# A linear-attention and MLP block on one core: tile 4 turned by moves, earlier normalisation of tiles 6 and 7, and other reorderings

## The chip, the core and the metric

The kernel runs on one core of a Trainium2 chip. The metric is the device time of one execution in microseconds. The engines work side by side, each in its own program order, and wait for each other by semaphores: TensorE (PE in the profile; its weight loads are PEld), VectorE (DVE), ScalarE (ACT), GpSimd (POOL) and SyncE (SP), which here issues nearly all transfers.

## What is computed

The input x is 2048 tokens by 512. With xn the layer-normalised x, the output is the sum of three parts:

```python
xn = _layernorm(x, axis=-1)
return x + _A_ref(xn, A_wqkv, A_wo) + _B_ref(xn, B_w1, B_b1, B_w2, B_b2)
```

A is linear attention with 32 heads of 16: q, k, v are xn times a 512 x 1536 matrix; phi(t) is t + 1 for positive t and exp(t) otherwise; for each head kv = phi(k)^T v and z = the sum of phi(k) over all tokens, and each token's output is phi(q) kv / (phi(q) z), times a 512 x 512 matrix. B is an MLP: the square of relu(xn w1 + b1), 1376 wide, times w2, plus b2. All is in float32.

## The kernel before

Tokens are worked in 16 tiles of 128, four tiles to a block. Every matmul of the accurate kind is done in three passes: an operand is split into a high part (rounded by a ScalarE or VectorE copy) and a low part (the difference, a subtraction), and high x high, high x low and low x high are accumulated. So each operand needs a copy on one engine and a subtraction on another before TensorE can use it.

The program order of each engine is the order in which the code issues its operations; there is no scheduler (a manual schedule). Names with numbers below are tiles of memory: xp is the normalised tile, pt its transpose in PSUM, xs0 and xs1 the transposed high and low parts (h and l) of two blocks, pk the projection of k and later its parts, k the value of phi, tok the normalised tile's parts, kx the accumulated product of tok and pk.

**First stage, the start (lines 516 to 655).** The first four tiles of x and the k weights are loaded. For each tile VectorE takes mean and variance (`measure`, lines 230 to 235), the root of the variance is made by an addition and a power (`roots`, lines 242 to 246: the addition on VectorE for tiles 0 and 1, else on GpSimd, the power on GpSimd), and `normalise` (248 to 273) writes xp: on VectorE for tiles under NPE = 8, later on ScalarE. A tile is turned in one of two ways:

- for tiles under NDVE = 5, by TensorE (`turned_pe`, line 303): four transposes with the identity into a PSUM bank pt, from which `high` (ScalarE, line 324), `low` (VectorE, line 327) and `keep_t` (a ScalarE copy, stored to DRAM as xTd for later) take their parts;
- for tiles from NDVE on, by moves: `regroup` (line 277) stores the normalised tile to DRAM (via), `move` (line 286) loads it back in four pieces in another order (xg), and `turn` (line 291) has VectorE transpose it within 32 x 32 blocks.

Before the token loop, tiles 0 to 3 are normalised; the loads of tiles 8 to 15 are issued together on SyncE; tiles 4 and 5 are measured as one group (`soon = group(4, 5)`), whose root is taken after the parts of tiles 0 and 1.

**The token loop (line 794 on), i from 2 to 15.** Each iteration issues the moves that are pending (`move()`, line 799), the projection of tile i (12 matmuls, line 369), phi of it (`phi_k`: two ScalarE passes, with the turned tile's `high` between them, then `low` and a VectorE pass), normalises the next group, splits k (`parts`, lines 372 to 377: a ScalarE copy and a VectorE difference) and the next tile's tokens (`tokens`: a ScalarE copy and a GpSimd subtraction), turns tile i + 2 by moves, measures later tiles, and ends with kx(i - 1): 12 matmuls (line 389) in three groups of four, ordered by which parts they need. At i = 5, four small loads of b1 are issued on SyncE (lines 796 to 798), ahead of the moves.

**Between token loop and main stage (lines 867 to 930).** Sums and differences of token blocks and of weight chunks are prepared for a product scheme in which TensorE needs fewer products than blocks: T[1] to T[4] are the token differences, S and aop the weight chunks' sums and parts. The heads' values and the matrix m are made from kx.

**Main stage (line 932 on).** For each half n (two blocks of four tiles) and each step p (a pair of 128-wide units of q or of the MLP, loop in line 1056) the code issues products into PSUM banks A, B and C, with ScalarE copies of A and C (c, t), the last sums' parts of T[3] and T[4] (`last_sums`, from line 1119), the weights' parts, and the second MLP product into acc. In step (0, 0) the parts of T[3] are made after the copy t of bank C.

Of the kernel before, what the change touches and what calls it, by code (L numbers as in the profile page):

```python
# [7 lines left out]
F32 = mybir.dt.float32  # L8
# [5 lines left out]
P = 128  # L14
# [4 lines left out]
def kernel(  # L19
# [39 lines left out]
    BT = TB * P  # L59
    NF = -(-F // P)  # L60
    NPE = 2 * TB
    NDVE = NPE - 3
    WARM = 11
    NP = NF // 2
    FP = NF * P
# [176 lines left out]
    def roots(tiles, st, mv, y):  # L242

        n = len(tiles)
        (nc.vector if tiles[0] < 2 else nc.gpsimd).tensor_scalar(y[:, 1, :n], mv[:, :n, 1], 1e-5, None, op0=OP.add)
        nc.gpsimd.tensor_tensor(out=y[:, 0, :n], in0=y[:, 1, :n], in1=power[:, :n], op=OP.pow)

    def normalise(tiles, st, mv, y):
# [96 lines left out]

        nc.gpsimd.memset(xp[i][:, D - 1:] if i < NDVE else xp[i][:, NJ - 1, P - 1:], 1.0)

    def tokens(i):
        tok[i] = pair(f"tok{i}")
        h, l = tok[i][:, 0], tok[i][:, 1]  # L350
        src = xp[i]
        if i >= NDVE:
            h, l, src = gjc(h), gjc(l), src.rearrange("p g (j c) -> p g j c", j=NJ)
        split(h, l, src, "act", "pool")
        if NDVE <= i + 1 < NT:
            ones(i + 1)

# [23 lines left out]
        phi(ps, kp[i], mid, late)  # L381

    def kx(i):
        second, third = ((1, 0), (0, 1)) if i < 2 else ((0, 1), (1, 0))
        order = (((1, 0),), ((0, 0), (0, 1))) if i >= NPE else (((0, 0),), (second,), (third,))
        todo = [(c, u, v) for group in order for c in range(NJ) for u, v in group]
        first, last = order[0][0], order[-1][-1]
        for c, u, v in todo:
            nc.tensor.matmul(kxp[c], lhsT=tok[i][:, u, c * P:(c + 1) * P], rhs=pk[i][:, v],  # L389
                             start=i == 0 and (u, v) == first, stop=i == NT - 1 and (u, v) == last)  # L390
# [155 lines left out]
    for i0 in range(0, NT, TB):  # L546
        a = first_xp[i0]
        for k in range(TB):
            xp[i0 + k] = a[:, k]
        if i0 + TB <= NDVE:  # L550
            continue
        n = TB if i0 >= NPE else TB // 2
        if i0 < NPE:
            i = i0 + TB - n - 1
            one = work.tile([P, 512], F32, name=f"xg{i}", tag="r0")
            xp[i], xg[i] = (t.rearrange("p (g n) -> p g n", g=NJ) for t in (xp[i], one))
            groups[i] = [xp[i], xg[i]]
# [27 lines left out]
    for t in two_tiles:  # L585
        measure(t)
        roots(*t)
    normalise(*two_tiles[0])
    high, low, keep0 = transposed(0, 2)
    high()  # L590
    heads_k(0, eng="dve")
# [47 lines left out]
    load_x(8, x8[:, :2])  # L639
    load_x(10, x8[:, 2:])  # L640
    load_x(12, two("x12"))
    load_x(14, two("x14"))
    project(2, pks[2], wk, HL)
    soon = group(4, 5)
    normalise(*fourth)
    phi_k(0, pks[0])
    measure(soon, 0)
    tokens(0)
    parts(0)
    phi_k(1, pks[1])  # L650
    tokens(1)
    measure(soon, 1)
    parts(1)
    roots(*soon)
    keep2()

# [135 lines left out]
    kxp = [bank(f"kx{c}", "acc") for c in range(NJ)]  # L792
    kx(0)
    for i in range(2, NT):
        if i == 5:
            nc.sync.dma_start(b1s[:, :NF - 1], b1[:(NF - 1) * P].rearrange("(f p) -> p f", p=P))
            for a, o, n in units(NF - 1):
                nc.sync.dma_start(b1s[a:a + n, NF - 1:], b1[o:o + n, None])
        move()
        if i in (4, 7):  # L800

            b = i // 7
            for u in range(2):
                nc.sync.dma_start(xsd[b][u], f32(cols(b * TB)[u]))
        if i == 9:
            load_o()
        if i > 10:
            fetch()
        ps = pks[i] if i < 3 else bank(f"pk{i}")
        if i > 2:  # L810
            project(i, ps, wk, HL)
        high = low = keep_t = lambda: None
        if i < NDVE:
            high, low, keep_t = transposed(i + 1)

        soon_turned = transposed(i + 2) if 11 <= i and i + 2 < NT else ()

        def mid():
            high()
            more(i)  # L820

        def late():
            low()
            more(i)

        if i == 12:
            rawz = raw_1(NF - 1)
            T.update({n: tokens_sum(n, f"B{n - 1}") for n in (1, 2)})
        if i == 12:
            w = load_1("q", 0)  # L830
        if i == 13:
            todo_1 = operands_first(0, w)
            extra.append(todo_1.pop(1))
        if i == 14:
            z = pair("w1z0")
            extra.append(lambda: split(z[:, 0], z[:, 1], rawz, "act", "dve"))
            o34 = halves(four("Tf", "r0"))
            extra.extend(sums_of(xT[NB - 1], xT[NB - 2], *o34))
            lows = [extra.pop() for k in range(2)]
            extra += [todo_1[0], lows[1], todo_1[1], lows[0], *todo_1[2:]]  # L840
        phi_k(i, ps, mid, late)
        more(i)
        run(*soon_turned)
        later = normalise(*soon) if soon else []
        parts(i)
        keep_t()
        if i == 2:
            tokens(2)
        if i + 1 < NT:
            tokens(i + 1)  # L850
        run(*later)
# [12 lines left out]
        kx(i - 1)  # L864
        more(i)
# [66 lines left out]
    for n in range(2):  # L932
# [118 lines left out]
        def step(k=1):  # L1051

            for _ in range(k):
                do(steps[t1] or steps[t2])

        for p in range(NO + 1):
            at_p = AT[p]
            kind, k = order[p] if p < NO else ("", 0)
# [22 lines left out]
            if kind:  # L1081
# [6 lines left out]
                if kind == "w":  # L1088
                    relu(c11, c11, fa)
                else:  # L1090
                    steps[t1] += steps_of(t1, fa, parts=True)
                step(at_p[0])
            if kind:
                if kind == "w":
# [20 lines left out]
            if p == NO:  # L1115
                break
            t5 = t5_
            if p == 0:
                def last_sums(k, *what):
                    for f in what:  # L1120
                        for j in range(2):
                            f(k, j, o34[k - 3][:, j])

                last_sums(3, difference_high, difference_low)
                if n == 0:
                    next_2(0)
            if p == 1:
                nc.vector.tensor_scalar(zc[:, 1], zc[:, 0], 1e-6, None, op0=OP.mult)
                acc = [bank(f"acc{t1}_{k}", "acc") for k in range(TB)]
# [229 lines left out]
```

## Time and profile before

| | |
|---|---|
| median of three runs | 412.59 us (411.94 to 412.9) |
| the profiled execution | 411.82 us, of which 410.1 us is the span from the first to the last instruction |
| mean granted TensorE clock | 0.999 |
| instructions | 5621 |
| TensorE, VectorE, ScalarE, GpSimd busy | 404.5, 303.2, 262.7, 48.7 us |

A timeline line gives start and length in us, the engine, the line of the kernel, the operation, what it writes and reads with the shape, how often, and in brackets how long the engine was idle before it and what ended that. Matmuls are pipelined: a 512-wide one is shown with some 0.39 us although the next one starts earlier, so starts are compared, not lengths. Transfers are listed with their size and the time from issue to landing.

### The profile page before, as it was taken

What the parts mean: (1) busy time and instruction counts of PE and PEld (TensorE: products, weight loads), DVE (VectorE), ACT (ScalarE), POOL (GpSimd) and SP (SyncE); (2) the same over time, 40 slices, a digit from 0 to 9 for tenths busy, and PEclk for the clock granted to TensorE, in tenths of its full rate; (3) what the DMA queues carried; (4) which work ended last, traced back from release to release, by engine and by line L of the source; (5) the groups of instructions that cost most, each with busy time, mean ns of one, the idle gap of its engine ahead of it and who ended that gap; (6) DMA issues with size and microseconds to landing.
All of it is one profiled execution on the core that took longest, in us unless ns stands there. A gap on an engine that the chain in (4) does not pass through costs nothing.

```text
span 410.1 us, 5621 instructions
## 1 busy us (share of the span) xinstructions
PE 404.5 (99%) x1947; PEld 332.3 (81%) x1947; DVE 303.2 (74%) x552; ACT 262.7 (64%) x460; POOL 48.7 (12%) x81
## 2 busy tenths in 40 slices
PE   8999999999999999999999999999999999999996
PEld 7888888888788888888878887888888888878885
DVE  5895567497798999988349957567989676449833
ACT  4756677456788789886818631677587857837520
POOL 5442333220000000030000200000000200000200
PEclk9999999999999999999999999999999999999999
DMA  6949676810342231381557992422121881034612
GB/s 212 351 151 331 187 308 205 246 37 0 95 114 79 77 102 27 104 203 28 207 215 248 335 201 104 114 53 51 51 78 34 238 189 29 2 104 151 104 26 102
DMA packets 46462, 56.34 MB, mean 137 GB/s; under 512 B 8225, under 2 KB 29985, under 8 KB 45154
## 3 DMA queue, kind: packets, MB, share of 16 engines
q1 hardware_dynamic: 44130, 51.80, 39.4%
q0 software_dynamic: 2304, 4.20, 6.4%
q8 instruction: 15, 0.25, 0.2%
q14 instruction: 13, 0.11, 0.1%
HBM read 41.43 MB, written 13.37 MB: 134 GB/s over the span
## 4 chain that ended last, share of the span: by engine, by line
PE 85%; DMA 6%; DVE 4%; ACT 2%; SPq 1%; issue 1%; ACTq 0%
PE b L488 31%; PE acc L130 28%; PE pk L369 11%; PE kx L389 10%; DMA r<-in_B_w_dram 5%; PE acc L499 2%; PE pz L130 1%; PE b L130 1%; DVE s L119 1%; DMA x<-in_A_x_dram 1%; PE pt L308 1%; SPq L207 0%; ACT aop L111 0%; ACT kxs L111 0%; ACT T L111 0%
## 5 line engine op out<-in xcount | busy, mean ns | idle before, releaser
L130 PE MATMUL acc<-w2r,s 128*128 128x512 f32 x477 | 113.1, 390 | 0.6 <-DVE s L119 0.6
L130 PEld LDWEIGHTS acc<-w2r,s 128*128 128x128 f32 x477 | 89.4, 188 | 20.3 <-DVE s L119 1.1
L488 PE MATMUL b<-T,aop 128*128 128x512 f32 x336 | 83.7, 390 | 0.2 <-ACT c L111 0.2
L488 PEld LDWEIGHTS b<-T,aop 128*128 128x128 f32 x336 | 62.8, 188 | 14.7 <-ACT t L111 0.8
L1037 POOL DMA_DIRECT2D res<-in_B_b_dram x16 | 14.4, 1108 | 278.7 <-DVE pt L429 86.7
L389 PE MATMUL kx<-pk,tok 128*128 128x512 f32 x192 | 46.5, 391 | 0.0
L389 PEld LDWEIGHTS kx<-pk,tok 128*128 128x128 f32 x192 | 35.8, 188 | 7.6 <-ACT pk L111 0.2
L488 PE MATMUL b<-xs0h,aop 128*128 128x512 f32 x112 | 36.9, 390 | 0.0
L130 PE MATMUL acc<-mh,aTsr 128*128 128x512 f32 x112 | 35.6, 389 | 0.0
L1045 DVE TENSOR_TENSOR res<-acc,res 128x512 f32<-128x512 f32 x16 | 11.0, 691 | 21.5 <-PE acc L130 19.2
L119 POOL TENSOR_TENSOR tok<-xp,tok 128x512 fp32r<-128x512 f32 x16 | 20.7, 1297 | 43.7 <-ACT tok L111 37.4
L488 PEld LDWEIGHTS b<-xs0h,aop 128*128 128x128 f32 x112 | 21.0, 188 | 4.4
L130 PEld LDWEIGHTS acc<-mh,aTsr 128*128 128x128 f32 x112 | 21.0, 188 | 4.4
L122 DVE TENSOR_TENSOR w2r<-r,w2r 128x512 fp32r<-128x512 f32 (+2 forms) x35 | 23.7, 680 | 0.1
L111 ACT ACTIVATE aop<-S 128x512 fp32r<-128x512 f32 x28 | 17.5, 624 | 9.8 <-DVE S L721 9.8
L119 DVE TENSOR_TENSOR aop<-S,aop 128x512 fp32r<-128x512 f32 x28 | 19.2, 686 | 4.8 <-ACT aop L111 4.4
L488 PE MATMUL b<-xs0l,aop 128*128 128x512 f32 x56 | 21.8, 389 | 0.0
L130 PE MATMUL acc<-ml,aTsr 128*128 128x512 f32 x56 | 21.8, 389 | 0.0
L119 DVE TENSOR_TENSOR s<-c,s 128x512 fp32r<-128x512 f32 x20 | 13.5, 688 | 11.2 <-ACT s L111 11.2
L111 ACT ACTIVATE w2r<-r 128x512 fp32r<-128x512 f32 x32 | 19.6, 619 | 2.7 <-DMA out_dram<-res 2.0
L111 ACT ACTIVATE T<-Tf 128x512 fp32r<-128x512 f32 x16 | 9.5, 624 | 16.1 <-DVE Tf L664 15.9
L488 PE MATMUL b<-xs1h,aop 128*128 128x512 f32 x56 | 19.5, 389 | 0.0
(189 smaller groups left out, 742.5 us busy)
## 6 DMA issues: line engine op xcount, KB each, us to landing
r<-in_B_w_dram SPq DMA_DIRECT2D x49, 256.0 KB, 3.0
res<-in_A_x_dram SPq DMA_DIRECT2D x8, 512.0 KB, 4.5
res<-in_B_b_dram POOLq DMA_DIRECT2D x16, 256.0 KB, 6.4
out_dram<-res SPq DMA_DIRECT2D x15, 256.0 KB, 2.1
via<-xp SPq DMA_DIRECT2D x5, 512.0 KB, 2.7
xg<-via SPq DMA_DIRECT2D x20, 128.0 KB, 2.7
xTd<-t SPq DMA_DIRECT2D x8, 256.0 KB, 4.3
x<-in_A_x_dram SPq DMA_DIRECT2D x4, 512.0 KB, 6.3
```

Of the source, the lines that this page charges most:

```text
L111: nc.scalar.activation(o, i, AF.Copy, bias=bias)
L119: ENG[el].tensor_tensor(out=l, in0=src, in1=f32(h), op=OP.subtract)
L122: nc.vector.tensor_tensor(out=l, in0=src, in1=f32(h), op=OP.subtract)
L130: nc.tensor.matmul(ps, lhsT=a[u], rhs=b[v], start=first and n == 0, stop=last and n == 2)
L308: nc.tensor.transpose(t[k][:, at:at + P], xp[i][:, j * P:(j + 1) * P], ident)
L369: nc.tensor.matmul(ps, lhsT=cols(i)[u][:, j, slot(i)], rhs=w[v][:, j, :], start=first and n == 0, stop=last and n == len(steps) - 1)
L389: nc.tensor.matmul(kxp[c], lhsT=tok[i][:, u, c * P:(c + 1) * P], rhs=pk[i][:, v], start=i == 0 and (u, v) == first, stop=i == NT - 1 and ( ...
L488: nc.tensor.matmul(ps, lhsT=a[u][:, j * P:(j + 1) * P], rhs=b[v][:, j, :], start=first and j == 0 and n == 0, stop=last and j == 1 and n == 2,
L499: nc.tensor.matmul(ps, lhsT=s[u][:, k * P:(k + 1) * P], rhs=w2s[NF - 1][u][:, a:z], start=first and u == 0, stop=stop and u == 1)
L1037: nc.gpsimd.dma_start(r[:, i], b2[None, :].partition_broadcast(P), accum_op=OP.add)
L1045: nc.vector.tensor_tensor(out=r[:, a:z], in0=ps, in1=r[:, a:z], op=OP.add)
```

## The change

- `NDVE` goes from 5 to 4: tile 4 is turned by moves and VectorE, no longer by TensorE. Its memory xg lies beside tile 5's.
- Tiles 4 and 5 are measured and rooted as two groups; tile 4 is normalised ahead of the token loop, with its DRAM store, and the load of tiles 14 and 15 is issued behind that store.
- The group of tiles 6 and 7 is normalised at the start of iteration 3's phi, behind tile 4's VectorE transpose, instead of after phi; the addition of its root is on VectorE.
- Tile 1's token copy is issued after its k parts, its low part is made by VectorE instead of GpSimd, and kx(1) takes its groups in the order of the later tiles (k's low part second, the tokens' low part third).
- Tile 0 is normalised in two halves of 256 columns.
- The b1 loads are issued at i = 13 instead of i = 5.
- In step (0, 0) of the main stage the parts of T[3] are made ahead of the copy t of bank C.

```diff
-    NDVE = NPE - 3
+    NDVE = NPE - 4
...
-        (nc.vector if tiles[0] < 2 else nc.gpsimd).tensor_scalar(y[:, 1, :n], mv[:, :n, 1], 1e-5, None, op0=OP.add)
+        (nc.vector if tiles[0] in (0, 1, 6) else nc.gpsimd).tensor_scalar(y[:, 1, :n], mv[:, :n, 1], 1e-5, None, op0=OP.add)
...
-    def tokens(i):
+    def tokens(i, el="pool"):
...
-        split(h, l, src, "act", "pool")
+        split(h, l, src, "act", el)
...
-        second, third = ((1, 0), (0, 1)) if i < 2 else ((0, 1), (1, 0))
+        second, third = ((1, 0), (0, 1)) if i < 1 else ((0, 1), (1, 0))
...
-            i = i0 + TB - n - 1
-            one = work.tile([P, 512], F32, name=f"xg{i}", tag="r0")
-            xp[i], xg[i] = (t.rearrange("p (g n) -> p g n", g=NJ) for t in (xp[i], one))
-            groups[i] = [xp[i], xg[i]]
+            single = work.tile([P, 2, 512], F32, name=f"xg{i0}s", tag="r0")
+            for k in range(2):
+                i = i0 + k
+                xp[i], xg[i] = (t.rearrange("p (g n) -> p g n", g=NJ) for t in (xp[i], single[:, k]))
+                groups[i] = [xp[i], xg[i]]
...
-    normalise(*two_tiles[0])
+    for k in range(2):
+        a = slice(k * D // 2, (k + 1) * D // 2)
+        nc.vector.tensor_scalar(xp[0][:, a], xr[0][:, a], two_tiles[0][2][:, 0, 0:1], two_tiles[0][3][:, 0, :1],
+                                op0=OP.subtract, op1=OP.mult)
...
-    load_x(14, two("x14"))
     project(2, pks[2], wk, HL)
-    soon = group(4, 5)
+    single = group(4)
+    soon = group(5)
     normalise(*fourth)
     phi_k(0, pks[0])
-    measure(soon, 0)
+    measure(single)
     tokens(0)
+    roots(*single)
     parts(0)
     phi_k(1, pks[1])
-    tokens(1)
-    measure(soon, 1)
+    normalise(*single)
+    load_x(14, two("x14"))
     parts(1)
+    tokens(1, "dve")
+    measure(soon)
     roots(*soon)
...
-        if i == 5:
+        if i == 13:
             nc.sync.dma_start(b1s[:, :NF - 1], b1[:(NF - 1) * P].rearrange("(f p) -> p f", p=P))
...
+        later = normalise(*soon) if i == 3 else []
...
-        later = normalise(*soon) if soon else []
+        if i != 3:
+            later = normalise(*soon) if soon else []
...
+                if (n, p) == (0, 0):
+                    last_sums(3, difference_high, difference_low)
                 step(at_p[0])
...
-                last_sums(3, difference_high, difference_low)
-                if n == 0:
-                    next_2(0)
+            if (n, p) == (0, 0):
+                next_2(0)
+            elif p == 0:
+                last_sums(3, difference_high, difference_low)
```

More of the change, by code (lines that the diff above doesn't have):

```diff
@@ L1054, in step, with last_sums @@
                 do(steps[t1] or steps[t2])
+        def last_sums(k, *what):
+            for f in what:
+                for j in range(2):
+                    f(k, j, o34[k - 3][:, j])
         for p in range(NO + 1):
@@ L1117 @@
             t5 = t5_
[L1118 to L1122, printed above, removed]
+            if (n, p) == (0, 0):
+                next_2(0)
+            elif p == 0:
                 last_sums(3, difference_high, difference_low)
-                if n == 0:
-                    next_2(0)
             if p == 1:
```

## The prediction

> **What bounds the kernel now.** I read the page first, then TensorE's waits (in total, times, the longest), then the chain in order of time, then the timelines at the places that the diff touches.
>
> ```profile
> PE 404.5 (99%) x1947; PEld 332.3 (81%) x1947; DVE 303.2 (74%) x552; ACT 262.7 (64%) x460; POOL 48.7 (12%) x81
> ```
> ```profile
> PE acc L130 <- DVE s L119: 0.6, 1, 0.6
> PE pk L369 <- ACT xs1h L324: 0.3, 1, 0.3
> PE b L488 <- ACT c L111: 0.2, 1, 0.2
> ```
> TensorE is busy for 404.5 of 410.1 us, and its waits past the first are three: 0.6, 0.3 and 0.2 us. So nothing can be won by making another engine quicker in general. Time goes only where TensorE waits, or where it issues something that isn't needed. The first token stage shows the undisturbed pace:
>
> ```profile
> 36.67 2.72 PE kx L389 x12
> ```
> Twelve 512-wide matmuls take 2.72 us, 0.227 each. Against that pace, here are the places that the change touches, from TensorE's timeline (start, length, then the instruction):
>
> ```profile
> 5.98 0.90 PE L308 MATMUL pt<-ident,xp 128*128 128x128 f32 x4
> 7.13 0.50 PE L369 MATMUL pk<-wkh,xs1h 128*128 128x512 f32 x1 [0.26 <-ACT xs1h L324]
> 7.47 0.60 PE L308 MATMUL pt<-ident,xp 128*128 128x128 f32 x4
> ...
> 25.14 0.60 PE L308 MATMUL pt<-ident,xp 128*128 128x128 f32 x4
> 25.50 3.02 PE L389 MATMUL kx<-pk,tok 128*128 128x512 f32 x12
> 28.35 0.39 PE L369 MATMUL pk<-wkh,xs0h 128*128 128x512 f32 x1
> ```
> ```profile
> 108.56 1.65 PE L488 MATMUL b<-T,aop 128*128 128x512 f32 x6
> ...
> 111.18 0.39 PE L488 MATMUL b<-xs1h,aop 128*128 128x512 f32 x1
> 111.78 1.66 PE L488 MATMUL b<-T,aop 128*128 128x512 f32 x6 [0.21 <-ACT c L111]
> 113.28 0.39 PE L488 MATMUL b<-xs0h,aop 128*128 128x512 f32 x1
> ```
>
> **The change part by part.** *Tile 4's transposes.* They leave TensorE. From 25.14 to 28.35 it needs 3.21 us for them and kx(2); kx(2) alone at the pace above is 2.72. **-0.49 us**, if tile 4's turned operand is there in time by the new way (below).
>
> *The third sum's parts.* TensorE finishes the last xs1h matmul's slot at 111.18 + 0.23 = 111.41, but starts only at 111.78, when ScalarE has copied bank A out (c, 111.13). Behind the wait the next six take 113.28 - 111.78 = 1.50 instead of 1.36. ScalarE works without a break from 107.59 to there:
>
> ```profile
> 107.59 0.60 ACT L111 ACTIVATE t<-b 128x512 f32<-128x512 f32 x1 [2.06 <-PE b L488]
> 108.09 1.15 ACT L111 ACTIVATE T<-Tf 128x512 fp32r<-128x512 f32 x2
> ...
> 111.13 0.60 ACT L111 ACTIVATE c<-b 128x512 f32<-128x512 f32 x1
> ```
> The change puts the two T copies ahead of t, into the 2.06 us in which ScalarE waits for TensorE. They depend on VectorE's differences alone, long made. Without them the rest moves up by about 1.0 us, and c can begin when the six matmuls of 108.56 are through, at 108.56 + 1.65 = 110.21; it ends at 110.8, 0.6 before TensorE asks. So the wait goes: 111.78 - 111.41 = 0.37, and 1.50 - 1.36 = 0.14 behind it: **-0.51 us**. VectorE's two T differences come sooner too and delay nobody.
>
> *Tile 0 in halves.*
>
> ```profile
> 5.39 0.54 DVE L268 TENSOR_SCALAR xp<-x,mv,y 128x512 f32<-128x512 f32 x1
> 5.84 0.42 DVE L115 CAST wkh<-rk 128x512 fp32r<-128x512 f32 x1
> 6.38 0.55 DVE L268 TENSOR_SCALAR xp<-x,mv,y 128x512 f32<-128x512 f32 x1
> 7.11 0.42 DVE L327 TENSOR_TENSOR xs1l<-pt,xs1h 128x256 fp32r<-128x256 f32 x1 [0.18 <-ACT xs1h L324]
> ```
> ```profile
> 5.55 0.80 POOL L246 TENSOR_TENSOR y<-y,power 128x1 f32<-128x1 f32 x1 [0.35 <-DVE y L245]
> ```
> ```profile
> 6.70 0.38 ACT L324 ACTIVATE xs1h<-pt 128x256 fp32r<-128x256 f32 x1 [4.62 <-PE pt L308]
> ```
> The first transposes start 0.05 after the 0.54 us normalisation. Half of it costs between 0.27 (half the time) and 0.42 (another 256-wide VectorE operation); I take 0.35. The first transpose then starts 0.19 sooner, ScalarE's copy 0.19 sooner, and the projection at 7.13 follows. The two halves together end some 0.1 later than the one did; the cast behind them ends at about 6.35, ahead of 6.9 when it is read, and tile 1's normalisation at 6.38 waits for GpSimd's 5.55 + 0.80 anyway. Bounds 0 and -0.19; I take **-0.17 us**, and all that hangs on this first projection moves along. The transposes of 5.98 take 0.90 us and those of 7.47 only 0.60, so TensorE's rate steps up between. By the Trainium skill (TensorE: Matmul & The Clock Gate, section "What's actually happening") that step comes from a free-running activity window, not from the work. Transposes moved ahead of it would then stay slow, and by that rule the start would give as little as nothing and the sum be -1.00; the two lengths agree with a step, and its moment in another execution isn't shown here.
>
> *Tile 1's tokens.* Of kx(1) the order becomes pk-low second, token-low third, and on ScalarE tile 1's token copy stands behind pk's, where tile 2's t copy stood:
>
> ```profile
> 18.21 0.63 ACT L111 ACTIVATE pk<-k 128x512 fp32r<-128x512 f32 x1 [0.23 <-DVE k L364]
> 18.75 0.58 ACT L111 ACTIVATE t<-pt 128x512 f32<-128x512 f32 x1
> ```
> All of this hangs on TensorE's projections, so with the 0.17 taken off the copy runs from 18.58 to 19.20; kx(1) wants it at 19.58 - 0.17 = 19.41 (the transposes of tile 3 lie ahead of it). Slack 0.2; cost nothing. VectorE's new token-low (0.69) is done by 20.0, wanted at 19.41 + 8 x 0.227 = 21.2. ScalarE then runs about one copy (0.5) later than before, and the next item adds to that.
>
> *Tile 4 by moves, tiles 6 and 7 sooner.*
>
> ```profile
> 21.70 1.00 DVE L268 TENSOR_SCALAR xp<-x,mv,y 128x512 f32<-128x512 f32 x2
> ...
> 25.52 0.18 DVE L235 BATCH_NORM_AGGREGATE mv<-st 128x2 f32<-128x6 f32 x1
> ...
> 30.08 0.71 DVE L293 STREAM_TRANSPOSE t<-xg 128x512 f32<-128x512 f32 x1
> ```
> ```profile
> 23.53 2.54 POOL L119 TENSOR_TENSOR tok<-xp,tok 128x512 fp32r<-128x512 f32 x2 [2.70 <-ACT tok L111]
> ...
> 26.35 0.72 POOL L246 TENSOR_TENSOR y<-y,power 128x2 f32<-128x2 f32 x1
> ```
> ```profile
> via<-xp SPq DMA_DIRECT2D x1, 256.0 KB, 2.1
> xg<-via SPq DMA_DIRECT2D x4, 64.0 KB, 1.9
> ```
> ```profile
> 11.50 3.93 SPq L159 DMA_DIRECT2D x<-in_A_x_dram  x4
> ...
> 24.83 1.75 SPq L289 DMA_DIRECT2D xg<-via  x4
> ```
> Tile 4's normalisation stands on VectorE right behind tile 1's k, which releases ScalarE's pk at 18.21 (18.04 now); so it is done at 18.5. SyncE then issues via (landing 2.1 later, 20.6; behind x12's load, the third of the four from 11.50 on, perhaps 21.3), x14's load, which nobody needs before tile 14, tile 2's t, and four moves (1.75 to issue, 1.9 to land): the last lands between 24.3 and, with x14's bytes before it, 25.3. Tile 5's via queues behind them and has time. VectorE's transpose, which waits for the moves, stands behind the three statistics whose last row ends at 25.70, and which now end some 0.15 later: it starts at about 25.9, so the moves have 0.6 to 1.6 us to spare. Behind it wait on VectorE all of tile 3's rest, and on ScalarE the high copy and tile 3's exponential. Transpose to 26.6, high copy (0.63) to 27.25. TensorE starts tile 4's projection at 28.35 - 0.17 - 0.49 = 27.69: slack 0.44. Its low part may come eight matmuls later.
>
> Behind the transpose VectorE now normalises tiles 6 and 7 (two for 0.91) ahead of tile 4's low part and tile 3's k. GpSimd's root for them follows the two token-lows: 26.4 to 27.1. So: normalised 28.0, low 28.65, k 29.3, ScalarE's pk 30.0; kx(3) wants it at 27.69 + 2.72 = 30.41. Slack 0.4. Cost nothing, with little left. Tile 5's transpose stands behind pk's low part, 30.7 to 31.4, its high copy ends at 32.1 and is wanted at 27.69 + 2 x 2.72 = 33.1. Tile 6's moves wait on SyncE for tile 5's turned copy: 31.4, 0.5 for that copy's issue, 1.75 and a landing within 3 (an estimate from 2.1 for 256 KB) make 36.7, turned and copied 38.0, wanted at 38.6. The lag isn't carried on, as the windows view shows (TensorE, its loads, VectorE, ScalarE, GpSimd):
>
> ```profile
> 25.00:97.00 72.00, 72.00 (x321) 59.63 (x320) 49.66 (x85) 44.45 (x75) 21.71 (x35) 1.00 0.61 198
> ```
> VectorE and ScalarE work 50 and 44 of the 72 us, so they catch up.
>
> *The b1 loads* leave SyncE's queue at tile 5, ahead of tile 8's moves, and go to tile 13:
>
> ```profile
> 77.15 3.25 SPq L707 DMA_DIRECT2D rq<-in_A_wqkv_dram  x2
> 89.09 1.57 SPq L207 DMA_DIRECT2D r<-in_B_w_dram  x3
> ```
> SyncE is idle from 80.40 to 89.09 there, and their first reader, the relu of the last unit, comes after kx(15). Cost nothing.
>
> **Sum:** -0.49 - 0.51 - 0.17 = -1.17 us. The profiled execution took 411.82 us for a span of 410.1, so 410.65 by it; it lies 0.77 below the median of the runs, 412.59, and from that I forecast **411.4 us**.
>
> **The rivals.**
> *A, a new wait in place of the old.* The slacks of 0.2 (token copy, kx(1)) and 0.4 (pk, kx(3)) are smaller than before. If one is missed by 0.3, TensorE loses that and about 0.14 behind it, as at 111.78: 411.85. For it: three engines in turn stand in each chain. Against: all of them are paced by TensorE, and move with it.
> *B, given back.* The 0.6 us wait of acc stands behind a crowd of transfers (the chain in order of time):
>
> ```profile
> 225.48 17.04 DMA r<-in_B_w_dram
> ```
> If these come no sooner, the wait grows by what was won: 412.6. Against: they are issued when TensorE lets buffers go, so they start sooner as well.
> *C, slower: tile 4's moves come late.* x14's load is issued between via and the moves, and x12's is still on its way.
>
> ```profile
> x<-in_A_x_dram SPq DMA_DIRECT2D x4, 512.0 KB, 6.3
> ```
> If via takes the 6.3 us of such a load rather than 2.1, it lands at 24.8, the last move at 28.5, high is ready at 29.9, and TensorE waits 2.2 us at 27.69: net +1.0, 413.6. TensorE begins to lose when the last move lands after 26.3, and the change is slower than before from 27.5 on. Against: via alone took 2.1, and x12, issued near 13.5, has most of its 6.3 us behind it at 18.5. By the Trainium skill (DMA: Bandwidth & Descriptors, "Queues, rings and completion order") one issuing engine's descriptors are consumed in ring order, which would put the moves behind x14's bytes; the 6.3 us against 2.1 fit that.
> *D, the third sum's move doesn't do what it says:* something else holds bank A or ScalarE up to 111.7, and 0.51 stays: 411.9. For it: ScalarE's row of copies has no gap, so one late input holds all of them. Against: t was released by TensorE, and the T copies need nothing of that time.
>
> **How the numbers follow.** Forecast 0.57 (its own range 410.6, the profiled execution less the sum, to 411.75, without the start's term and a bit of A); A 0.17; B 0.08; C 0.10; D 0.08. About 0.2% (0.8 us) is what a measurement of this kernel can tell from no change. The forecast is faster than that; A, D and most of B lie within; C and a little of B are slower: 0.57, 0.31, 0.12. The range goes from 410.6 to 412.6, which takes in all but C and half of B.
>
> **What would show it.** Right: 16 transposes instead of 20 on TensorE; kx(2) to the projection of tile 4 in 2.72; no wait on c near 111; the first projection at about 6.96; the wait of acc still about 0.6. Wrong: a wait at tile 4's first projection on ScalarE's xs0h with a DMA behind it (C), one at kx(1) or kx(3) (A), or a larger wait at acc (B).

## The result, and the profile after

The changed kernel takes **410.41 us** (median of 9 runs, 409.81 to 411.37), the kernel before beside it 412.57 (9 runs, 411.41 to 412.98): ratio **0.9959**, 95% interval 0.9946 to 0.9972. It is faster by about 0.4%. Run twice more, on other chips, it gave 0.9964 (0.9949 to 0.9979) and 0.9981 (0.9966 to 0.9995); these two are e8 and e12 below. The forecast was 411.4 us, 0.9971 of the 412.59 that it started from. The median of 410.41 lies 0.2 below the range's lower end; 0.9959 of 412.59 would be 410.9, inside it.

The profiled execution of the changed kernel took 410.41 us with a span of 408.7 (before: 411.82 and 410.1). The span is 1.41 us shorter. Where it went is seen from landmarks on TensorE, as starts in us from the span's start. The right-hand columns are two later profiled executions of the same changed kernel:

| stretch | before | after | change | after, e8 | after, e12 |
|---|---|---|---|---|---|
| to VectorE's first instruction (tile 0 has landed) | 3.36 | 3.43 | +0.07 | 3.57 | 3.48 |
| from there to kx(0) | 13.04 | 12.84 | -0.20 | 13.07 | 12.97 |
| kx(0) to kx(2) | 9.10 | 8.67 | -0.43 | 8.76 | 8.77 |
| kx(2) to tile 5's projection | 8.29 | 8.53 | +0.24 | 8.27 | 8.26 |
| tile 5's projection to the heads' values | 68.09 | 68.14 | +0.05 | 68.09 | 68.73 |
| heads' values to the matmul 41 behind m's values (118.38, 117.49) | 16.50 | 15.88 | -0.62 | 15.90 | 15.88 |
| from there to the last matmul's end, without the step at the acc wait | 287.19 | 287.16 | -0.03 | 287.19 | 287.17 |
| the step at the acc wait, start to start | 1.02 | 0.80 | -0.22 | 0.46 | 1.49 |
| last matmul's end to the span's end | 3.53 | 3.26 | -0.27 | 3.25 | 3.24 |

The step at the acc wait was 0.45 to 1.49 us in the fourteen profiled executions of all kernels here, without order: it is scatter of one execution, and the -0.22 is no gain of the change. Of the other eight lines, three repeat in all three profiles of the change: kx(0) to kx(2), 0.33 to 0.43 less; the heads' values to the matmul behind m's, 0.60 to 0.62 less; and the end, 0.27 to 0.29 less.

The page's first part and TensorE's waits (total, times, longest), after:

```profile
PE 403.8 (99%) x1943; PEld 331.7 (81%) x1943; DVE 304.7 (75%) x556; ACT 262.2 (64%) x459; POOL 48.5 (12%) x81
```
```profile
PE acc L130 <- DVE s L119: 0.4, 1, 0.4
PE pt L308 <- DVE xp L591: 0.2, 1, 0.2
PE pk L369 <- ACT xs1h L324: 0.2, 1, 0.2
```
Four instructions are missing on TensorE: tile 4's transposes. The wait on c has left the list; the wait for xs1h, the first projection's, is 0.2 instead of 0.3.

**The start.** TensorE's timeline, after:

```profile
5.91 0.76 PE L308 MATMUL pt<-ident,xp 128*128 128x128 f32 x4 [0.17 <-DVE xp L591]
6.82 0.50 PE L369 MATMUL pk<-wkh,xs1h 128*128 128x512 f32 x1 [0.15 <-ACT xs1h L324]
7.19 0.66 PE L308 MATMUL pt<-ident,xp 128*128 128x128 f32 x4
```
The first projection stood at 7.13 and stands at 6.82, though tile 0 landed 0.07 later. The four transposes take 0.76 instead of 0.90. TensorE's rate had already stepped up, and the last two wait for the second half of tile 0: the third starts at 6.23, and that half (5.77, 0.41 long) ends at 6.18. Behind it tile 1's transposes take 0.66 instead of 0.60.

**The third sum.** TensorE, then ScalarE, after:

```profile
108.29 1.65 PE L488 MATMUL b<-T,aop 128*128 128x512 f32 x6
...
110.92 0.39 PE L488 MATMUL b<-xs1h,aop 128*128 128x512 f32 x1
111.14 1.52 PE L488 MATMUL b<-T,aop 128*128 128x512 f32 x6
112.50 0.39 PE L488 MATMUL b<-xs0h,aop 128*128 128x512 f32 x1
```
```profile
105.16 1.14 ACT L111 ACTIVATE T<-Tf 128x512 fp32r<-128x512 f32 x2
107.33 0.60 ACT L111 ACTIVATE t<-b 128x512 f32<-128x512 f32 x1 [1.02 <-PE b L488]
...
110.10 0.60 ACT L111 ACTIVATE c<-b 128x512 f32<-128x512 f32 x1
```
The T copies stand in ScalarE's gap, c ends at 110.70, and TensorE goes from 110.92 to 111.14 and on to 112.50 at 0.22 to 0.23 each, without a wait.

**Tile 4.** The matmuls of kx(2) and tile 4's projection on TensorE, after:

```profile
24.94 2.88 PE L389 MATMUL kx<-pk,tok 128*128 128x512 f32 x12
27.89 0.50 PE L369 MATMUL pk<-wkh,xs0h 128*128 128x512 f32 x1
28.23 0.39 PE L369 MATMUL pk<-wkl,xs0h 128*128 128x512 f32 x1
```
From kx(2) to the projection are 2.95 us, not the 2.72 of twelve matmuls, and the next start is 0.34 away instead of 0.23: a new wait of 0.23, and 0.11 behind it. The chain that leads to it, on SyncE, VectorE and ScalarE:

```profile
18.49 0.34 SPq L281 DMA_DIRECT2D via<-xp  x1
18.89 0.43 SPq L159 DMA_DIRECT2D x<-in_A_x_dram  x1
19.67 0.52 SPq L336 DMA_DIRECT2D xTd<-t  x1
20.92 3.66 SPq L289 DMA_DIRECT2D xg4s<-via  x4
```
```profile
25.68 0.63 DVE L245 TENSOR_SCALAR y<-mv 128x2 f32<-128x2 f32 x1
26.46 0.71 DVE L293 STREAM_TRANSPOSE t<-xg4s 128x512 f32<-128x512 f32 x1 [0.15 <-DMA xg4s<-via]
```
```profile
27.21 0.63 ACT L324 ACTIVATE xs0h<-t 128x512 fp32r<-128x512 f32 x1 [1.47 <-DVE t L293]
```
via is issued at 18.49 as forecast and lands at 20.85. The four moves take SyncE 3.66 us to issue instead of 1.75, since the second is held up from 21.30 to 23.62. The load of tiles 14 and 15, issued at 18.89, lands at 24.91; the last move lands at 26.34, 1.43 behind it. VectorE waits for it by 0.15, and TensorE loses 0.23.

**The end.** After the last landing the span still went on for 1.20 us before and for 0.91 after. SyncE's last checks of the DMAs' semaphores (us, start and end, from the trace; before on the left, after on the right):

```
408.94 408.97 semaphore 103          407.06 407.09 semaphore 107
409.00 409.03 semaphore 104          407.44 407.47 semaphore 108
409.06 409.09 semaphore 106          407.82 407.84 semaphore 109
409.12 409.15 semaphore 107          407.88 407.89 drain
409.18 409.21 semaphore 108
409.24 409.27 semaphore 109
409.31 409.31 drain
```
Eight semaphores (101 to 104 and 106 to 109) are given to SyncE's DMAs in turn, and at the end they are checked in this fixed order. Before, the last store to land carried 103, and five more checks of 0.06 us followed. After, it carries 109, the last in the order. Tile 4's way by moves issues five DMAs more (via and four moves), so every later DMA has a semaphore five places on.

### The profile page after: what moved, and what is told of

Same layout as the page of the kernel before. It is cut to its first block, busy times and chain, and to the rows that moved or that the text cites. A ratio compares the mean times of both kernels' runs of the same rounds, so it can differ in the third digit from the quotient of the medians.

```text
span 408.7 us, 5630 instructions
## 1 busy us (share of the span) xinstructions
PE 403.8 (99%) x1943; PEld 331.7 (81%) x1943; DVE 304.7 (75%) x556; ACT 262.2 (64%) x459; POOL 48.5 (12%) x81
## 4 chain that ended last, share of the span: by engine, by line
PE 85%; DMA 6%; DVE 5%; issue 1%; SPq 1%; ACT 1%; POOL 1%; DVEq 0%; ACTq 0%
PE b L488 33%; PE acc L130 29%; PE pk L369 9%; PE kx L389 9%; DMA r<-in_B_w_dram 4%; PE acc L499 2%; PE pz L130 1%; DVE s L119 1%; SPq L289 1%; PE b L130 1%; PE pz0b L130 1%; DMA x<-in_A_x_dram 1%; DMA via<-xp 1%; DMA xg4s<-via 1%; PE pt L308 0%
## 5 line engine op out<-in xcount | busy, mean ns | idle before, releaser
L119 POOL TENSOR_TENSOR tok<-xp,tok 128x512 fp32r<-128x512 f32 x15 | 19.8, 1322 | 38.9 <-ACT tok L111 38.9
```

Of the source, the lines that this page charges most:

```text
L119: ENG[el].tensor_tensor(out=l, in0=src, in1=f32(h), op=OP.subtract)
```

## The experiments

Twelve kernels, in three groups of four, each group on a chip of its own beside 35 runs of the kernel before, whose median was 412.14, 412.0 and 411.93 us. A ratio is to those runs. **Theory**: the gain is the third sum's wait, tile 4's transposes, part of tile 0's halves and the shorter end; the load of tiles 14 and 15 ahead of tile 4's moves gives some of it back. **Rivals**: the account of one execution is scatter; the parts lose elsewhere what they win; the end is chance.

**e1, the third sum alone**, in the kernel before:

```diff
+                if (n, p) == (0, 0):
+                    last_sums(3, difference_high, difference_low)
                 step(at_p[0])
```


> The kernel before with only the third sum's parts moved ahead of the copy t. Theory: the wait on c near 111 and what follows it go, the span is shorter by 0.5 to 0.65 us, and the wait of acc near 249 keeps its size: ratio to before near 0.9986. Rival: the gain is given back at the wait of acc, because the crowd of transfers ahead of it doesn't come sooner: ratio 1.000, with that wait at 1.1 us instead of 0.6.

411.31 us, ratio 0.9981 (0.9968 to 0.9994). From the heads' values to the matmul 41 behind m's values 15.88 us instead of 16.50: **-0.62**, as in the whole change. TensorE:

```profile
111.35 0.39 PE L488 MATMUL b<-xs1h,aop 128*128 128x512 f32 x1
111.58 1.52 PE L488 MATMUL b<-T,aop 128*128 128x512 f32 x6
```
0.23 from start to start: no wait, and nothing given back up to the acc wait.

**e2, tile 0 in halves alone**, in the kernel before:

```diff
-    normalise(*two_tiles[0])
+    for k in range(2):
+        a = slice(k * D // 2, (k + 1) * D // 2)
+        nc.vector.tensor_scalar(xp[0][:, a], xr[0][:, a], two_tiles[0][2][:, 0, 0:1], two_tiles[0][3][:, 0, :1],
+                                op0=OP.subtract, op1=OP.mult)
```


> The kernel before with only tile 0 normalised in two halves. Theory: first projection 0.2 to 0.3 us sooner, of which about 0.2 is left when kx(0) starts, since tile 1's normalisation waits for GpSimd and so tile 1's transposes come no sooner: ratio 0.9995. Rival: all is given back in the first 20 us and nothing is left: ratio 1.000.

411.52 us, ratio 0.9991 (0.9976 to 1.0007): too little for the runs to show. In the profile, from VectorE's first instruction the first projection comes after 3.39 us instead of 3.77, and kx(0) after 12.79 instead of 13.04. So 0.38 is won at the first projection and **0.25** is left at kx(0). In this execution TensorE's quick rate had come ahead of the transposes, in the profile before it had not; how much of the 0.25 is owed to that is not shown.

**e3, the change without the third sum:**

```diff
-                if (n, p) == (0, 0):
-                    last_sums(3, difference_high, difference_low)
```
(and the old place restored.)

> The changed kernel with the third sum's parts put back behind the copy t. Theory: the wait on c near 111 is back with about 0.2 shown and 0.5 to 0.65 us longer in all than the changed kernel: ratio to before 0.9975 to 0.998. Rival, that it stands for most of the measured gain: ratio near 0.999.

412.08 us, ratio 0.9992 (0.9975 to 1.0008): the rival's ratio, while the theory's 0.9975 to 0.998 lies at the interval's edge, so the runs leave it open whether the third sum stands for most of the gain. The profile speaks for the theory's size of that part. The stretch from the heads' values is 16.53 again. kx(2) to tile 4's projection is 2.72 here, without a wait, which the theory hadn't foreseen: the load of tiles 14 and 15 landed at 24.43 and the last move at 25.84. The end behind the last landing is 0.90.

**e4, the load of tiles 14 and 15 behind tile 4's moves**, in iteration 3:

```diff
-    load_x(14, two("x14"))
+    x14 = two("x14")
...
+        if i == 3:
+            load_x(14, x14)
```


> The changed kernel with the load of tiles 14 and 15 issued behind tile 5's moves instead of between tile 4's store and moves. Theory: the second move is no longer held up in SyncE for 2.3 us, the moves land near 24 instead of 26.3, VectorE's transpose starts when its queue lets it (26.3 at the latest) and TensorE's wait at tile 4's projection shrinks from 0.34 to 0.1 or less: 0.25 to 0.34 us shorter than the changed kernel. Rival: VectorE's queue (the addition of 0.63 us behind GpSimd's token-lows) is what holds the transpose, and the wait stays at 0.2 or more.

411.03 us, ratio 0.9981 (0.9966 to 0.9996), not better than the changed kernel's. The wait at tile 4 is gone (2.72), but a new one of 0.42 us stands at kx near 81, behind tile 12's moves, which were issued at 73.67 instead of 71.00. The k weights also came late in this execution, so its start is no evidence.

**e5, the same load only in iteration 6:**

```diff
-    load_x(14, two("x14"))
+    x14 = two("x14")
...
+        if i == 6:
+            load_x(14, x14)
```


> The changed kernel, with the load of tiles 14 and 15 issued only in iteration 6, behind that iteration's moves. Theory (this load stood ahead of tile 4's moves and made them late): the wait at tile 4's first projection goes, from kx(2)'s start to that projection 2.72 us instead of 2.95 and the stretch behind it undisturbed, so 0.25 to 0.34 us less than the changed kernel, about 410.1 us, ratio to the kernel before 0.995; and no wait at tile 12, because via and moves of tiles 6 to 9 no longer queue beside the load. Rival (the whole chain of via and moves has no room for 512 KB more anywhere): a wait of 0.3 to 0.5 us appears at a later tile, and the time is that of the changed kernel, 410.4 us.

410.62 us, ratio 0.9966 (0.9949 to 0.9983). No wait at tile 4 (25.33 to 28.05 is 2.72) and none at tile 12; the last move landed at 25.32. But e8 beside it, with the load where the change has it, had no wait either and took as long. The mechanism is shown, the gain is not.

**e6, three DMAs more**, by splitting the first b1 load of the changed kernel in four:

```diff
-            nc.sync.dma_start(b1s[:, :NF - 1], b1[:(NF - 1) * P].rearrange("(f p) -> p f", p=P))
+            for f, z in ((0, 3), (3, 6), (6, 8), (8, NF - 1)):
+                nc.sync.dma_start(b1s[:, f:z], b1[f * P:z * P].rearrange("(f p) -> p f", p=P))
```


> The changed kernel, with b1's first load split into four, so that SyncE issues three DMAs more and the last store carries another semaphore of the eight that are used in turn. Theory (SyncE checks the eight in a fixed order at the end, some 0.06 us each, and the last store's was the last in that order): five more checks follow the last landing, the span ends 1.2 us after it instead of 0.9, and the kernel takes 0.3 us longer, 410.7 us; nothing else moves. Rival (the shorter end is scatter of one profiled execution): the end stays at 0.9 us and the time at 410.4 us.

410.72 us, ratio 0.9969 (0.9951 to 0.9986). The last store carries 103 again, five checks follow its own (408.39 to 408.66, then the drain at 408.69), and the span ends **1.21** us after the last landing. In all fourteen profiles it is 1.20 to 1.22 where the last store has 103 (before, e1, e2, e6) and 0.89 to 0.91 where it has 109 (the other ten). So the 0.3 us at the end are not scatter. In the runs' medians (410.72 against e8's 410.63) they can't be told from nothing. Tile 4's projection waits in this profile too, by 0.26.

**e7, tile 4's part alone** (with tiles 6 and 7 and tile 1's tokens; the other three parts undone):

```diff
-    for k in range(2):
...
+    normalise(*two_tiles[0])
...
-        if i == 13:
+        if i == 5:
...
-                if (n, p) == (0, 0):
-                    last_sums(3, difference_high, difference_low)
```


> Tile 4 by moves, tiles 6 and 7 sooner and tile 1's tokens, without the third sum's parts, tile 0's halves and the b1 move. Theory: TensorE loses the transposes (0.43 less from kx(0) to kx(2)), gets 0.24 to 0.34 back at tile 4's first projection, keeps the wait on c near 111 (16.5 us from m's values to the block after it, as before), and the program's end is 0.3 us shorter because of the five more DMAs: in all 0.4 us less than the kernel before, 411.7 to 412.1 us, ratio 0.999. Rival (tile 4's move is worth its full 0.49 us): ratio 0.998 or less.

411.2 us, ratio 0.9973 (0.9956 to 0.9989). Here my theory fell and the rival held: the expected 0.999 lies just outside the interval. From kx(0) to tile 4's projection 11.52 us instead of 11.95, so **-0.43** with no wait, and the end is 0.89. These two make 0.7 us (0.9982), which is the rival's ratio and lies in the interval. The wait at tile 4 is not a fixed price of the change.

**e8, the changed kernel again.**

> The changed kernel once more, as the yardstick for the runs beside it. Theory: ratio 0.996; the wait at tile 4's first projection (0.2 to 0.3 us), the shorter end (0.9 us after the last landing) and the missing wait on c are there again; the wait of acc near 248 us falls anywhere between 0.4 and 1.1 us start to start. Rival (some of these are scatter of one execution): one of the first three is gone or changed by over 0.15 us.

410.63 us, ratio 0.9964 (0.9949 to 0.9979). The end (0.90) and the missing wait on c (15.90) are there again. The wait at tile 4's projection is not, as its rival had it. TensorE and SyncE:

```profile
25.40 2.88 PE L389 MATMUL kx<-pk,tok 128*128 128x512 f32 x12
28.12 0.47 PE L369 MATMUL pk<-wkh,xs0h 128*128 128x512 f32 x1
```
```profile
21.26 2.63 SPq L289 DMA_DIRECT2D xg4s<-via  x4
```
2.72: the load of tiles 14 and 15 landed at 24.33 instead of 24.91, the moves' issue was held up by 1.0 us less, and the last move landed at 25.67, again 1.3 behind the load. Something else is new, at tile 2's statistics on VectorE:

```profile
8.93 0.69 DVE L234 BATCH_NORM_STATS2 st<-x 128x6 f32<-128x512 f32 x1 [0.28 <-DMA x<-in_A_x_dram]
```
Tile 2's load landed at 8.91 (8.14 in the first profile after), and kx(0) began 7.73 us later. The same 7.73 to 7.74 stands in e5, e6 and e7, whose tile 2 landed at 8.81, 8.90 and 9.15: the start has a second bound.

**e9, tile 2's load ahead of the last k weights:**

```diff
-    load_k(*range(NJ))
+    load_k(0, 1, 2)
     t = two("x2")
-    for i in range(2):
-        load_x(2 + i, t[:, i:i + 1])
+    load_x(2, t[:, :1])
+    load_k(3)
+    load_x(3, t[:, 1:])
```


> The changed kernel, with the load of tile 2 issued ahead of the last of the four k-weight loads instead of behind it. In four profiles kx(0) began 7.73 us after tile 2's load landed, in the others 8.1 or more after it. Theory (a second bound of the start: tile 2's load, whose landing varies between 8.05 and 8.91 us, holds VectorE's statistics and through them kx(0)): tile 2 lands some 0.65 us sooner, kx(0) no longer lies 7.73 behind it but 8.3 or more, and begins 12.8 us after VectorE's first instruction whatever the loads do; where the loads are late that is 0.25 us won, where they are early nothing: 410.2 to 410.5 us. Rival (the last weights are needed as soon): a wait for the weights near 9 us, and kx(0) as late or later than 13.1 us after VectorE's first instruction.

Tile 2 lands at 7.95, VectorE doesn't wait for it, and kx(0) comes 12.83 us after VectorE's first instruction (8.51 after the landing). The theory of the start holds. Yet the kernel took 411.53 us, ratio 0.9984 (0.997 to 0.9998), no better than e12 beside it: a larger wait appeared elsewhere. VectorE and TensorE, e9:

```profile
79.19 0.71 DVE L293 STREAM_TRANSPOSE xT<-xg 128x512 f32<-128x512 f32 x1 [6.58 <-DMA xg<-via]
```
```profile
81.28 0.70 PE L389 MATMUL kx<-pk,tok 128*128 128x512 f32 x2 [1.22 <-ACT pk L111]
```
Tile 12's last move landed at 79.00 (75.17 in the first profile after), and TensorE lost 1.38 us. All four kernels of this group have the wait: 1.38, 0.98, 0.46 and 0.53.

**e10, the two edits undone that were costed at nothing:**

```diff
-        second, third = ((1, 0), (0, 1)) if i < 1 else ((0, 1), (1, 0))
+        second, third = ((1, 0), (0, 1)) if i < 2 else ((0, 1), (1, 0))
...
+    tokens(1)
     parts(1)
-    tokens(1, "dve")
...
-        if i == 13:
+        if i == 5:
```


> The changed kernel, with the two edits undone that were costed at nothing: tile 1's low tokens from GpSimd again and in the old order, and b1's loads at i = 5. Theory (both cost nothing): TensorE's starts from kx(0) to kx(2) and from tile 5's projection on stay within 0.1 us of the changed kernel's, and the time is 410.5 us, ratio to the kernel before 0.996. Rival (one of them carried a part of the gain): a wait of 0.2 us or more at kx(1), at tile 4's projection or behind i = 5, and 410.8 us or more.

411.06 us, ratio 0.9979 (0.9966 to 0.9992), the same time as e12. In the profile the rival is right: the wait at tile 4's projection is now 0.48, the largest of all. VectorE, GpSimd and TensorE, e10:

```profile
18.11 1.54 DVE L268 TENSOR_SCALAR xp<-x,mv,y 128x512 f32<-128x512 f32 x1
```
```profile
18.07 1.30 POOL L119 TENSOR_TENSOR tok<-xp,tok 128x512 fp32r<-128x512 f32 x1
```
```profile
25.15 2.88 PE L389 MATMUL kx<-pk,tok 128*128 128x512 f32 x12
28.35 0.50 PE L369 MATMUL pk<-wkh,xs0h 128*128 128x512 f32 x1 [0.31 <-ACT xs0h L324]
```
Tile 1's low tokens on GpSimd run beside tile 4's normalisation on VectorE, which takes 1.54 us; in the changed kernel GpSimd is free then, and it takes 0.55:

```profile
17.92 0.55 DVE L268 TENSOR_SCALAR xp<-x,mv,y 128x512 f32<-128x512 f32 x1
```
via goes out at 19.68 instead of 18.49, the last move lands at 26.80, and TensorE waits. Here the four moves were issued in 1.76 us, without being held up, and the last still landed 1.50 behind the load of tiles 14 and 15.

The Trainium skill (SBUF — State Buffer, section "SBUF: two separate sides") has GpSimd and VectorE share a port pair as an exclusive lock. The trace agrees: GpSimd began 0.04 us earlier and ended at 19.37, and VectorE ended at 19.65. As 256 columns of such a normalisation take 0.41 us and 512 take 0.55, I estimate that the columns themselves take 0.28 of the 0.55, and 0.28 is just what VectorE still needed when GpSimd had ended.

The b1 loads at i = 5 are not seen to cost anything. A loss of 0.19 around 39.44 in this profile is not in e12's, but e4, with b1 at 13, has 0.20 there, and before and e7, with b1 at 5, have none.

**e11, e9's and e5's edits together.**

> The changed kernel with both repairs: tile 2's load ahead of the last k weights, and the load of tiles 14 and 15 in iteration 6. Theory (the two waits that are left in the token stage, up to 0.25 us at kx(0) and up to 0.34 us at tile 4's projection, depend on when loads land, and both go): from VectorE's first instruction to tile 4's projection 24.2 us (12.84 to kx(0), 8.67 to kx(2), 2.72 on), the least of any profile so far being 24.37; 410.0 to 410.3 us. Rival (both are scatter that other waits take over): no difference to the changed kernel, 410.5 us.

The token stage does what the theory says, to the hundredth: from VectorE's first instruction (3.46) to tile 4's projection 24.20 us. TensorE:

```profile
24.94 2.88 PE L389 MATMUL kx<-pk,tok 128*128 128x512 f32 x12
27.66 0.49 PE L369 MATMUL pk<-wkh,xs0h 128*128 128x512 f32 x1
```
The time says the opposite: 411.81 us, ratio 1.001 (0.9994 to 1.0027), by the ratio the slowest of the twelve. The profiled execution, with 410.55, is the quickest of its twelve runs, so its profile doesn't show what the others lost. It has the wait at tile 12 too (0.46). What the rest is stays open.

**e12, the changed kernel a third time.**

> The changed kernel as the yardstick beside these three. Theory: ratio 0.996; kx(0) 12.8 us after VectorE's first instruction if tile 2's load lands before 8.4 us, and 7.73 us after that landing otherwise; at tile 4's projection a wait only if the last of tile 4's moves lands less than 1.6 us ahead of kx(2)'s start plus 2.72. Rival (these two don't decide): kx(0) or tile 4's projection against one of the two rules by over 0.1 us.

410.76 us, ratio 0.9981 (0.9966 to 0.9995). kx(0) began 7.73 us after tile 2's landing (8.72), and no wait stood at tile 4 (last move 25.72, 2.22 ahead of the due time): both rules hold. But 0.53 us were lost at tile 12:

```profile
78.18 0.71 DVE L293 STREAM_TRANSPOSE xT<-xg 128x512 f32<-128x512 f32 x1 [5.73 <-DMA xg<-via]
```
```profile
80.27 0.93 PE L389 MATMUL kx<-pk,tok 128*128 128x512 f32 x3 [0.37 <-ACT pk L111]
```
In the kernel before the same transpose stood in time, but by little:

```profile
77.65 0.71 DVE L293 STREAM_TRANSPOSE xT<-xg 128x512 f32<-128x512 f32 x1 [4.92 <-DMA xg<-via]
```
It needs to start 2.1 us ahead of kx: in e4, e9, e10, e11 and e12 it started 1.69, 0.72, 1.12, 1.65 and 1.56 ahead, and with the loss each makes 2.1. Before, kx was due at 80.03 and the transpose started 2.38 ahead. So the kernel before has 0.3 us of slack there. Whether it waits on that third chip as well is not shown: its profile is from another group. Tile 12's moves stand on SyncE right ahead of the loads of wv and wvl and three of r, as tile 4's stand beside the load of tiles 14 and 15. What made them late on that chip is not shown, but which part was: the trace counts each landing in sixteen updates of its semaphore, and of tile 12's last move in e12 fifteen had come by 76.50 and the sixteenth at 77.98 (75.14 and 75.17 in the first profile after).

## Why the prediction was right, and where its sizes were off

The direction and the class were right: faster, by 0.4% where 0.3% was forecast. The largest term was the one it named. Step by step:

- **The third sum's parts, -0.51 us:** right in mechanism, -0.60 to -0.62 in four profiles (after, e1, e8, e12). The 0.11 more is mostly a second small stumble, near 117.7, that hung on the same wait and that I had not counted. Rival D is out.
- **Tile 4's transposes, -0.49:** right in size as far as tile 4's projection. From kx(1) to there it is 8.77 us before and 8.28 to 8.30 in the seven profiles in which the moves were in time (e3, e4, e5, e7, e8, e11, e12). From there to tile 5's projection 0.07 to 0.12 is given back (5.51 to 5.56 instead of 5.44), most of it behind the first matmul, so -0.38 is left.
  The step that failed is the slack: "the moves have 0.6 to 1.6 us to spare", "slack 0.44". Two things took it. First, the addition for the root of tiles 6 and 7, which the change puts on VectorE ahead of tile 4's transpose, takes 0.63 us beside GpSimd's token subtractions and ends 0.06 behind them (after, e3, e12); at tile 0, with one column instead of two, it takes 0.15. The transpose needs to start 1.43 us ahead of the projection's due time (kx(2)'s start plus 2.72), and in the seven profiles it starts 1.43 to 1.49 ahead. Nothing is left to spare. Second, the moves land not between 24.3 and 25.3 but between 25.67 and 26.89 wherever the load of tiles 14 and 15 is ahead of them, 1.2 to 1.5 behind that load, as the table shows. I had put 1.0 us of it on the moves, and in rival C let via pay the rest; but via was quick (2.4 us). TensorE begins to lose when the last move lands less than 1.55 us ahead of the due time (forecast: 1.39). So C is real, small, and there in some executions only. That the load makes the moves late is shown: with it the last landing comes 1.07 to 2.45 us ahead of the due time, without it (e4, e5, e11) 2.73 to 2.93. What holds the issue up on SyncE is not shown, since the four took 2.60 us in e11 without the load and 1.76 in e10 with it.
- **Tile 0 in halves, -0.17:** 0.20 to 0.25 at kx(0) where tile 2's load is in time, but not by the forecast's way alone. A half took 0.41, near the upper bound of 0.42, so the first transpose comes 0.14 sooner behind VectorE's first instruction (2.48 against 2.62) and not 0.19. The first projection gained 0.38 all the same (3.39 against 3.77), because the sum took TensorE's rate as given. In e7, which has no halves, the transposes happened to be quick, and the first projection came after 3.53; so at the quick rate halves are worth 0.14, and the rest is rate. By the rule of the Trainium skill that the prediction weighed (TensorE: Matmul & The Clock Gate, section "What's actually happening") the step's moment is not the kernel's to choose. Its moment does vary here. In before and e1 the first transposes still step at 0.21 us from start to start; in e3, e6, e7, e8, e9 and e12 even the warm-up matmuls ahead of them step at 0.11. In all eleven profiles with halves the quick rate had come by the second transpose, and the first projection came after 3.39 to 3.43; what halves are worth when it comes later is not shown. The gain at kx(0) is only there if tile 2's load is in time. In ten profiles with halves kx(0) begins, to 0.04 us, at the later of two times: 12.83 us after VectorE's first instruction, or 7.73 us after tile 2's landing (the eleventh is e4, whose weights came late). With landings from 8.8 on nothing is left of the gain (e5, e6, e8).
- **Tile 1's tokens, 0:** right as a cost, and incomplete. It is what keeps GpSimd off VectorE while tile 4 is normalised (e10). In e10's one profile the wait at tile 4 is 0.48, where the changed kernel's three have 0.23 and twice none; by the runs e10 and e12 can't be told apart.
- **Tiles 6 and 7 sooner, and b1, 0:** neither kx(1) nor kx(3) was late in any profile of the change, so rival A is out. B would have added what was won to the step of 1.02 at the acc wait; it falls between 0.45 and 1.49 for kernels of either kind, so B is out as well.
- **What the sum left out, -0.27 to -0.3:** I counted tile 4's five new DMAs in SyncE's queue but not in the turn of the semaphores, and so in the end of the program.

The figures behind tile 4's wait, in us: when the load of tiles 14 and 15 and the last of tile 4's moves landed, how far ahead of the projection's due time VectorE's transpose started, and what TensorE lost there.

| profile | load lands | last move lands | transpose ahead by | TensorE loses |
|---|---|---|---|---|
| after | 24.91 | 26.34 | 1.20 | 0.23 |
| e3 | 24.43 | 25.84 | 1.47 | 0 |
| e6 | 25.45 | 26.89 | 1.17 | 0.26 |
| e7 | 25.15 | 26.69 | 1.49 | 0 |
| e8 | 24.33 | 25.67 | 1.45 | 0 |
| e9 | 25.29 | 26.52 | 1.22 | 0.21 |
| e10 | 25.30 | 26.80 | 0.95 | 0.48 |
| e12 | 24.45 | 25.72 | 1.44 | 0 |

Undisturbed, the sum is thus -0.25 - 0.38 - 0.62 - 0.3 = -1.55 us (0.9962) instead of -1.17. Up to 0.25 at tile 4, 0.25 at kx(0) and 0.5 at tile 12 (if the kernel before doesn't lose that too) are lost in executions in which loads land late. That fits the three ratios from 0.9959 to 0.9981. Part of the nearness of 0.9971 to 0.9959 is luck: in the first profile after, the 0.3 at the end that the sum left out stands against the 0.25 lost by the wait at tile 4 that it left out too. The raw medians differ by 2.16 us, more than this sum; but the interval of the ratio, 0.9946 to 0.9972, allows 1.2 to 2.2, so the runs don't tell the two apart.

No kernel here beats the changed one: each repair of one late landing (e4, e5, e9, e11) worked in its place, and none made the whole faster.

## What to carry to other kernels

A transfer on the path must be priced with what is in flight and queued on the same engine, and its slack compared with the scatter of landings, not with one execution's. What stands ahead of the waiting instruction on its own engine takes from that slack too. An edit that costs nothing may be what keeps a neighbour cheap: before dropping it, look for what would then run beside the moved instruction on the engine that it frees. Where gains are tenths of a microsecond, cut the span into stretches between landmarks in several executions of the same kernel; only lines that repeat are gains.

## What the runs showed of the hardware

- At the end of the program SyncE checks eight DMA semaphores in a fixed order at 0.06 us each. How many of SyncE's DMAs the program has decides which semaphore the last store carries, and with it up to 0.3 us of the end (0.89 to 0.91 against 1.20 to 1.22 us in fourteen profiles).
- The last of four 64 KB moves issued behind a 512 KB load on SyncE landed 1.2 to 1.5 us behind that load in eight profiles. Their issue took 1.76 to 3.66 us in these, 1.75 in the kernel before, and 2.60 in e11 without that load.
- In the latest landings it was the last of a transfer's sixteen parts that was late: of the load of tiles 14 and 15 fifteen had come by 23.35 and the sixteenth at 25.29 us in e9, by 23.19 and at 25.45 in e6 (by 23.66 and at 24.33 in e8).
- A 128x512 normalisation on VectorE took 0.55 us alone and 1.54 us beside a 1.30 us GpSimd subtraction that began 0.04 sooner; it ended 0.28 after the subtraction. An addition of 128x2 took 0.63 us there beside GpSimd's subtractions, and one of 128x1 without them 0.15.
- TensorE's step from 0.21 us to 0.11 from start to start of 128x128 matmuls came at different times: near 3.7 us in e6, near 6.5 us before, and after 6.6 us in e1.
